# Which queue loads what in the first microseconds of a fused S5 + SwiGLU kernel on Trainium2

## The chip, the cores and the metric

The kernel runs on one core of one Trainium2 chip. A core has TensorE (PE, matrix products), VectorE (DVE), ScalarE (ACT, activation functions), GpSimd (POOL) and SyncE (SP, which here only issues DMA transfers), each with its own instruction stream. SP, ScalarE and GpSimd can each issue DMA transfers, and each has its own DMA queue. The metric is device time in microseconds (us) of one execution; the time before is the median of three runs.

## The reference

The kernel computes a layer norm of x (2048 rows of 512, bf16), and on the result a state-space layer (S5) and a SwiGLU feed-forward layer; x and both results are added.

```python
def _A_ref(x, Lambda_re, Lambda_im, B_re, B_im, C_re, C_im, log_dt, Dskip):
    Lam = Lambda_re + 1j * Lambda_im
    Bmat, Cmat = B_re + 1j * B_im, C_re + 1j * C_im
    Lam_bar = jnp.exp(jnp.exp(log_dt) * Lam)
    B_bar = ((Lam_bar - 1.0) / Lam)[:, None] * Bmat
    Bu = jnp.einsum("bld,pd->blp", x + 0j, B_bar)
    h = jnp.zeros_like(Bu[:, 0, :])
    hs = []
    for t in range(L):
        h = Lam_bar[None, :] * h + Bu[:, t, :]
        hs.append(h)
    y = 2.0 * jnp.einsum("blp,dp->bld", jnp.stack(hs, 1), Cmat).real
    return y + x * Dskip[None, None, :]

def _B_ref(x, w_gate, w_up, w_down):          # (512, 1376), (512, 1376), (1376, 512)
    return (silu(x @ w_gate) * (x @ w_up)) @ w_down

x = A_x
xn = _layernorm(x, axis=-1)
return x + _A_ref(xn, ...) + _B_ref(xn, ...)
```

Inputs and output are bf16; matrix products accumulate in f32.

## The kernel before, in words

The 2048 rows are 16 row tiles of 128, and four chunks of 512 columns of the transposed activations. The gate and up weights have 1376 columns, eleven blocks of 128 (the last of 96). They are loaded in groups of blocks: group 0 holds blocks 0 and 1, group 1 blocks 2 and 3, group 2 blocks 4 to 6, group 3 blocks 7 to 9; the last block has tiles of its own, `w_last` and `wu_last`. Everything is written in a fixed order (a manual schedule), so each engine runs its instructions in the order in which the program writes them.

For each chunk, TensorE does the gate and up products (L418), the B projection (L343), and later the down projection (L498) and the state-space output (L507). ScalarE evacuates the results from PSUM: silu on the gate (L432), a copy of the up product (L433), a copy of the B projection (L345). VectorE multiplies gate and up (L437), runs the scan and the rotations (L353 to L385) and computes the norm statistics. PSUM has eight banks, which the tiles take in turn: a tile waits until the tile eight before it has been read out.

The first 14 us are different, because nothing can start before rows, weights and norm are there. This is called the head here. The loads at its beginning (L115 to L122, with `load_w1` at L112) are split over SP's and ScalarE's queues: row tiles x0 to x3 one by one, 128 KB each, and groups 0 and 1 of gate and up, 256 KB each. After them SP issues the next four row tiles, groups 2 and 3, eight transposing loads of B, and `w_last`. Later, `load_late` (L140) puts `wu_last`, the last eight row tiles and the down weights on SP's queue. Eight semaphores are handed to these DMA transfers in turn, across both queues, and a transfer isn't issued before the earlier one with its semaphore has landed. So the ninth transfer (the next four row tiles) and those behind it wait for the head's first loads.

While the first rows load, TensorE runs `dummy` matmuls on a zero tile (L566), which keep it busy. Then, row tile by row tile: VectorE takes the statistics (L174, L599, L614), the reciprocal standard deviation comes from ScalarE's Ln and Exp for x0 (L179, L180) and from VectorE and GpSimd for the others (L183, L184), VectorE normalises (L192), TensorE transposes (L207), ScalarE copies the transposed rows to SBUF (L215; VectorE L213 for x3), and TensorE multiplies them with the first three weight blocks (`head_mm`, L591). The order at L598 to L625 interleaves the tiles; on VectorE, x1's statistics (L599) stand ahead of x0's normalisation (L600). Ln and Exp need ScalarE's function table, which is loaded once at L595; a second table load comes at L245. The pieces that the text speaks of:

```python
    allk = range(KD)
    nc.scalar.preload_act_table_set("natural_log_exp_and_others")
    dummy(10, CW)
    ln_stats(0)
    rstd_act(0)
    nc.vector.bn_stats(out=stats[:, 1, :], in_=xall[:, 1, :])
    norm_dve(0)
    ...
    xT_pe(0, 2)
    dummy(6, 128)
```

Of the kernel before, what the change touches and what calls it, by code (L numbers as in the profile page):

```python
# [23 lines left out]
def kernel(  # L24
# [17 lines left out]
    nc = tc.nc  # L42
    _, L, D = A_x.shape
    Pst = A_Lambda_re.shape[0]
    F = B_w_gate.shape[1]
    assert L % 512 == 0 and D % 128 == 0 and Pst % 128 == 0 and Pst == D
    CW = 512
# [11 lines left out]
    LA, LB = 32, 64  # L59
    FL = (FT - 1) * 128  # L60
# [18 lines left out]
    x_v = A_x[0].rearrange("(n p) d -> p n d", p=128)  # L79
    out_v = out[0].rearrange("(n p) d -> p n d", p=128)  # L80
    wg_v = B_w_gate.rearrange("(k p) f -> p k f", p=128)
    wu_v = B_w_up.rearrange("(k p) f -> p k f", p=128)


    xall = const.tile([128, NT, D], BF16, name="xall")
# [9 lines left out]
    wu_last = const.tile([128, KD, LB], BF16, name="wu_last")  # L95
# [14 lines left out]
    def load_w1(q, tiles, view, gi):  # L110
        a, b = fgroups[gi]
        q.dma_start(out=tiles[gi][:], in_=view[:, :, a * 128:min(F, b * 128)])  # L112


    nc.sync.dma_start(out=xall[:, 0, :], in_=x_v[:, 0, :])  # L115
    nc.scalar.dma_start(out=xall[:, 1, :], in_=x_v[:, 1, :])
    load_w1(nc.sync, wg_g, wg_v, 0)
    load_w1(nc.scalar, wu_g, wu_v, 0)
    nc.sync.dma_start(out=xall[:, 2, :], in_=x_v[:, 2, :])
# [18 lines left out]
    nc.sync.dma_start(out=w_last[:, :, LB + LA:128], in_=wu_v[:, :, FL:FL + LA])  # L138

    def load_late():  # L140
        nc.sync.dma_start(out=wu_last[:], in_=wu_v[:, :, FL + LA:F])
        nc.sync.dma_start(out=xall[:, 2 * TPC:NT, :], in_=x_v[:, 2 * TPC:NT, :])
        nc.sync.dma_start(out=wd_sb[:, 0:nfull, :], in_=B_w_down[0:nfull * 128, :].rearrange("(k p) d -> p k d", p=128))
        if nfull < FT:
            nc.sync.dma_start(out=wd_sb[0:LB, nfull, :], in_=B_w_down[FL + LA:F, :])
            nc.sync.dma_start(out=wd_sb[LB:LB + LA, nfull, :], in_=B_w_down[FL:FL + LA, :])
# [26 lines left out]
    def ln_stats(n):  # L173
        nc.vector.bn_stats(out=stats[:, n, :], in_=xall[:, n, :])  # L174
        nc.vector.bn_aggr(out=mv[:, n, :], in_=stats[:, n, :])
# [388 lines left out]
    def dummy(n, cols):  # L564
        for _ in range(n):
            nc.tensor.matmul(warm[:, 0:cols], lhsT=junk[:, 0:128], rhs=junk[:, 0:cols], start=True, stop=True)  # L566
# [25 lines left out]
                                 rhs=xnT[:, k, lo * 128:hi * 128], start=(k == 0), stop=(k == KD - 1))  # L592

    allk = range(KD)
    nc.scalar.preload_act_table_set("natural_log_exp_and_others")  # L595
    dummy(10, CW)
    ln_stats(0)
    rstd_act(0)  # L598
    nc.vector.bn_stats(out=stats[:, 1, :], in_=xall[:, 1, :])  # L599
# [101 lines left out]
    spread(fwd0[8:] + back0, norm2, "ssm0", "ln2")  # L701
    queue("cf", c_ops())
    load_late()
    for fi in range(G0, FT):
        gateup_tile(0, fi)
# [60 lines left out]
```

## Time and profile before

| what | value |
|---|---|
| time, median of 3 runs | 180.59 us (180.54 to 180.66) |
| the profiled execution's own time | 180.64 us |
| its span in the profile | 178.9 us |
| granted TensorE clock | 1.00 of full speed |
| PE busy | 174.0 us (97%), 919 matmuls |
| VectorE busy | 153.2 us (86%) |
| ScalarE busy | 93.8 us (52%) |
| GpSimd busy | 24.9 us (14%) |
| SP's queue (q1) | 24416 packets, 11.21 MB |
| ScalarE's queue (q10) | 1632 packets, 0.89 MB |
| read from HBM | 8.03 MB |

The span is the time from the first to the last instruction of the program that the profile shows; the rest of the execution's own time lies around it. The busy time of PE counts each matmul with a modelled end, so PE "busy" is not PE at its peak. A timeline line gives start and duration in us, the engine, the line of the kernel, the operation and its tiles; an engine with a q behind its name (SPq, ACTq) is that engine's queue issuing a DMA transfer, and the duration is that of the issue, not of the transfer. In square brackets stand the idle time before the instruction and what ended it. "To landing" is the time from the issue to the moment when the transfer's semaphore tells that all of it has arrived.

### The profile page before, as it was taken

The numbers are of one execution on the slowest core, as the hardware profiler recorded it, in microseconds if no ns is written. First come the engines' busy times: TensorE is split into PE (matmuls) and PEld (weight loads), VectorE is DVE, ScalarE is ACT, GpSimd is POOL, SyncE is SP. The second block draws the span as 40 slices with busy tenths as digits, with TensorE's granted clock in tenths as the row PEclk, the third lists the DMA queues.
The fourth block names the chain that finished last, engine by engine and source line by source line (L and its number), as shares of the span: only waits on it lengthen the run. The fifth ranks groups of instructions, "written<-read, shape, count | busy, mean of one in ns | idle before, by whom it ended". The sixth has DMA issues, their size and how long they took to land.

```text
span 178.9 us, 2463 instructions
## 1 busy us (share of the span) xinstructions
PE 174.0 (97%) x919; PEld 83.5 (47%) x919; DVE 153.2 (86%) x233; ACT 93.8 (52%) x170; POOL 24.9 (14%) x32
## 2 busy tenths in 40 slices
PE   7899999999999999999999999999999999999993
PEld 2684444443444444444444444444444444444743
DVE  2779997999999999999999999999999999950033
ACT  2479776988399957022998661014866610230000
POOL 5223000000500000027200000013405000150000
DMA  5999857994236500020930000007287900073012
GB/s 164 319 274 211 116 97 184 353 171 96 52 64 180 235 0 0 0 28 7 133 71 2 0 0 4 0 0 76 25 134 101 137 3 0 0 81 36 4 47 70
DMA packets 29515, 15.53 MB, mean 87 GB/s; under 512 B 18336, under 2 KB 29440, under 8 KB 29472
## 3 DMA queue, kind: packets, MB, share of 16 engines
q1 hardware_dynamic: 24416, 11.21, 27.3%
q0 software_dynamic: 3456, 3.28, 14.1%
q10 hardware_dynamic: 1632, 0.89, 1.8%
q8 instruction: 7, 0.11, 0.3%
q14 instruction: 4, 0.03, 0.0%
HBM read 8.03 MB, written 5.24 MB: 74 GB/s over the span
## 4 chain that ended last, share of the span: by engine, by line
PE 95%; DMA 2%; DVE 1%; ACT 0%; issue 0%
PE ps L418 36%; PE ps L498 21%; PE ps L507 15%; PE ps L343 15%; PE ps L591 3%; PE ps L444 2%; DMA xall<-in_A_x_dram 2%; PE ps L454 1%; PE ps L207 1%; DVE stats L174 0%; DVE stats L599 0%; DVE xall L192 0%; ACT xnT L215 0%; PE ps L566 0%; DVE res L510 0%
## 5 line engine op out<-in xcount | busy, mean ns | idle before, releaser
L498 PE MATMUL ps<-wd_sb,guT 128*128 128x512 bf16 (+3 forms) x198 | 38.8, 355 | 0.0
L418 PE MATMUL ps<-xnT,wg 128*128 128x512 bf16 x148 | 38.0, 379 | 0.0
L418 PE MATMUL ps<-xnT,wu 128*128 128x512 bf16 x148 | 38.0, 379 | 0.0
L385 DVE TENSOR_TENSOR_SCAN g<-r_t,car,u 128x512 bf16<-128x512 f32 x24 | 28.9, 1266 | 0.0
L507 PE MATMUL ps<-CF,wt 128*128 128x512 bf16 (+2 forms) x144 | 28.3, 355 | 0.0
L343 PE MATMUL ps<-xnT,BT 128*128 128x512 bf16 x128 | 28.3, 379 | 0.0
L498 PEld LDWEIGHTS <-guT 128*128 128x128 bf16 (+1 forms) x198 | 18.5, 98 | 19.9
L513 ACT CAST res<-ps 128x512 bf16<-128x512 f32 x12 | 7.0, 586 | 38.3 <-PE ps L507 38.3
L432 ACT ACTIVATE guT<-ps 128x512 bf16<-128x512 f32 x40 | 24.8, 620 | 3.6 <-PE ps L418 3.4
L433 ACT CAST u<-ps 128x512 bf16<-128x512 f32 x40 | 24.3, 607 | 4.1 <-PE ps L418 4.0
L514 POOL DMA_DIRECT2D out_dram<-res x12 | 11.1, 998 | 87.2 <-ACT res L513 87.2
L418 PEld LDWEIGHTS <-wu 128*128 128x128 bf16 x148 | 14.5, 98 | 17.4
L418 PEld LDWEIGHTS <-wg 128*128 128x128 bf16 x148 | 14.3, 98 | 17.6 <-issue 0.8
L507 PEld LDWEIGHTS <-wt 128*128 128x128 bf16 x144 | 13.4, 98 | 14.3
L343 PEld LDWEIGHTS <-BT 128*128 128x128 bf16 x128 | 12.5, 98 | 15.1
L345 ACT CAST u<-ps 128x512 bf16<-128x512 f32 x32 | 17.6, 590 | 2.9 <-PE ps L343 2.8
L510 DVE TENSOR_TENSOR res<-ps,xn_end 128x512 bf16<-128x512 f32 (+2 forms) x6 | 3.0, 514 | 14.4 <-PE ps L507 14.4
L437 DVE TENSOR_TENSOR guT<-guT,u 128x1024 bf16<-128x1024 bf16 x20 | 13.6, 682 | 0.0
L184 POOL TENSOR_TENSOR rstd<-ve,neg_half 128x1 f32<-128x1 f32 (+1 forms) x6 | 6.9, 1154 | 40.2 <-DVE ve L183 40.2
L174 DVE BATCH_NORM_STATS2 stats<-xall 128x6 f32<-128x512 bf16 x14 | 9.4, 670 | 2.4 <-DMA xall<-in_A_x_dram 2.4
L353 DVE TENSOR_TENSOR pm<-u,c 128x2048 bf16<-128x2048 bf16 x8 | 9.8, 1221 | 1.2 <-ACT c L270 1.1
L353 DVE TENSOR_TENSOR pm<-g,c 128x2048 bf16<-128x2048 bf16 x8 | 9.8, 1219 | 0.1
(103 smaller groups left out, 156.8 us busy)
## 6 DMA issues: line engine op xcount, KB each, us to landing
out_dram<-in_A_x_dram SPq DMA_DIRECT2D x1, 1536.0 KB, 8.5
out_dram<-res POOLq DMA_DIRECT2D x12, 128.0 KB, 3.0
out_dram<-xall POOLq DMA_DIRECT2D x3, 512.0 KB, 5.5
wd_sb<-in_B_w_down_dram SPq DMA_DIRECT2D x1, 1280.0 KB, 10.9
xall<-in_A_x_dram SPq DMA_DIRECT2D x1, 1024.0 KB, 6.5
wg<-in_B_w_gate_dram SPq DMA_DIRECT2D x2, 384.0 KB, 5.5
wu<-in_B_w_up_dram SPq DMA_DIRECT2D x2, 384.0 KB, 5.9
wu<-in_B_w_up_dram ACTq DMA_DIRECT2D x2, 256.0 KB, 5.3
```

Source lines behind the costliest of these rows:

```text
L174: nc.vector.bn_stats(out=stats[:, n, :], in_=xall[:, n, :])
L343: nc.tensor.matmul(ps[:], lhsT=BT[:, part, k, q * 128:(q + 1) * 128], rhs=xnT[:, k, c * CW:(c + 1) * CW], start=(k == 0), stop=(k == KD - 1))
L345: nc.scalar.copy(out=u_tiles[c][:, part, q, :], in_=ps[:])
L353: V.tensor_tensor(out=t[:], in0=flat(src()[:, i]), in1=flat(tab[:]), op=ALU.mult)
L385: V.tensor_tensor_scan(out=g()[:, part, q, :], data0=r_t[:, q:q + 1].to_broadcast([128, CW]), data1=u_tiles[c][:, part, q, :], initial=ini ...
L418: nc.tensor.matmul(ps[:fs, lo:hi], lhsT=wslice(groups, fi, k), rhs=xnT[:, k, c * CW + lo:c * CW + hi], start=(k == 0), stop=(k == KD - 1))
L432: nc.scalar.activation(out=guT[:fs, fi, :], in_=psg[:fs], func=ACT.Silu)
L433: nc.scalar.copy(out=u_pair[c][:fs, fi % 2, :], in_=psu[:fs])
L437: products.append(lambda: V.tensor_tensor(out=g, in0=g, in1=u, op=ALU.mult))
L498: nc.tensor.matmul(o[:], lhsT=gu_tiles[c][:fsz[fi], fi, i * 128:(i + 1) * 128], rhs=wd_sb[:fsz[fi], fi, lo:hi], start=(fi == 0), stop=False)
L507: nc.tensor.matmul(o[:], lhsT=w_tiles[c][:, part, q, i * 128:(i + 1) * 128], rhs=CF[:, part, q, lo:hi], start=False, stop=(part == 1 and q ...
L514: nc.gpsimd.dma_start(out=out_v[:, n, lo:hi], in_=res[:, lo:hi], accum_op=ALU.add)
```

## The change

The head's loads are shared out differently. The table load moves from behind ScalarE's four load issues to the very front of its stream, x1 moves from ScalarE's queue to SP's, behind x0, and so SP issues x0, x1, gate group 0, x2, gate group 1 and ScalarE issues, after the table load, up group 0, x3, up group 1. In `load_late`, `wu_last` moves from SP's queue to ScalarE's; in the built program its issue stands between the last copy of the first B projection (L345) and the silu of block 7 (L432) in ScalarE's stream. Nine dummy matmuls of 512 columns run instead of ten.

```diff
+    nc.scalar.preload_act_table_set("natural_log_exp_and_others")
     nc.sync.dma_start(out=xall[:, 0, :], in_=x_v[:, 0, :])
-    nc.scalar.dma_start(out=xall[:, 1, :], in_=x_v[:, 1, :])
+    nc.sync.dma_start(out=xall[:, 1, :], in_=x_v[:, 1, :])
     load_w1(nc.sync, wg_g, wg_v, 0)
     load_w1(nc.scalar, wu_g, wu_v, 0)
     nc.sync.dma_start(out=xall[:, 2, :], in_=x_v[:, 2, :])
...
     def load_late():
-        nc.sync.dma_start(out=wu_last[:], in_=wu_v[:, :, FL + LA:F])
+        nc.scalar.dma_start(out=wu_last[:], in_=wu_v[:, :, FL + LA:F])
         nc.sync.dma_start(out=xall[:, 2 * TPC:NT, :], in_=x_v[:, 2 * TPC:NT, :])
...
     allk = range(KD)
-    nc.scalar.preload_act_table_set("natural_log_exp_and_others")
-    dummy(10, CW)
+    dummy(9, CW)
     ln_stats(0)
```

## The prediction

> **What bounds the kernel now.** I read the busy time per stage first, then the chain that ended last, then the first 10 us of the timeline. TensorE (windows of the whole trace; after the window: its length, PE busy and count, clock, DMA share, GB/s):
>
> ```profile
> 4.60:5.60 1.00, 0.30 (x4) 1.00 1.07 280
> 6.80:7.80 1.00, 0.88 (x17) 1.00 1.07 320
> 7.80:9.80 2.00, 2.00 (x28) 1.00 1.09 350
> 12.00:60.00 48.00, 48.00 (x241) 1.00 0.77 166
> 60.00:120.00 60.00, 60.00 (x279) 1.00 0.13 23
> 120.00:176.00 56.00, 56.00 (x300) 1.00 0.38 53
> ```
>
> From 7.8 us to 176 us TensorE never pauses, so the end moves only with the moment at which that run begins, or if something makes it pause. The chain (start, us, what) says what sets that moment:
>
> ```profile
> 0.74 2.78 DMA xall<-in_A_x_dram
> 3.54 0.70 DVE stats L174
> 4.27 0.18 DVE mv L175
> 4.45 0.59 DVE stats L599
> 5.05 0.42 DVE xall L192
> 5.52 0.40 PE ps L207 x4
> ...
> 11.25 1.86 PE ps L591 x32
> 13.11 6.91 PE ps L418 x32
> ```
>
> It is the landing of x0, the first 128 rows, at 0.74 + 2.78 = 3.52 us; then statistics, ScalarE's Ln and Exp (beside x1's statistics), norm, transposes: 2.00 us from landing to the first transpose. The timeline has the issues and the consumers:
>
> ```profile
> 0.74 0.41 ACTq L116 DMA_DIRECT2D xall<-in_A_x_dram  x1
> 0.74 0.40 SPq L115 DMA_DIRECT2D xall<-in_A_x_dram  x1
> 1.18 0.46 ACTq L112 DMA_DIRECT2D wu<-in_B_w_up_dram  x1
> 1.20 0.41 SPq L112 DMA_DIRECT2D wg<-in_B_w_gate_dram  x1
> 2.77 1.28 ACT L595 ACT_TABLE_LOAD   x1 [2.77 <-issue]
> 4.49 0.29 ACT L179 ACTIVATE ve<-mv,eps_t 128x1 f32<-128x1 f32 x1 [0.43 <-DVE mv L175]
> ...
> 28.58 2.64 SPq L145 DMA_DIRECT2D wd_sb<-in_B_w_down_dram  x1
> 30.95 0.57 ACT L345 CAST u<-ps 128x512 bf16<-128x512 f32 x1
> 31.42 0.60 ACT L432 ACTIVATE guT<-ps 128x512 bf16<-128x512 f32 x1
> ```
>
> x0 and x1 leave at the same time on two queues and share the DMA engines; the table load ends at 4.05, before L179 needs it.
>
> **The change part by part.** The sum is made on the profiled execution: 180.64 us = span 178.9 + 1.74 around it; it lies 0.05 above the median, 180.59.
>
> x1 to SP, behind x0: this is the gain. Windows of the DMA give 14, 154 and 360 GB/s in 1.5 to 2.0, 2.0 to 2.5 and 2.5 to 3.0 us: 7 + 77 + 180 = 264 kB, which is x0 and x1 together (262 kB), done at about 3.0. Had x0 these bytes to itself, its 131 kB would be there at 2.5 + 47/360 = 2.63: 0.37 us earlier, landing at 3.15. A second row gives the same: the 64 KB loads on a quiet queue late in the trace (w_last, wu_last) land 2.2 us after issue; 66 kB more at 350 GB/s add 0.19, so 2.39 instead of 2.78, or 0.39. The lower end is 0: the up group takes x1's place beside x0 (if the table load doesn't hold its issue, below). I take 0.37, because in the only place of this trace where ScalarE's loads and a table load meet, the load begins 0.03 us after the last issue ends (2.29 + 0.46 = 2.75; 2.77): one after the other.
>
> Table load to the front: removed where it was free (2.77 to 4.05 with L179 waiting for L175 until 4.45). With x0's chain 0.37 earlier, L175 would be done at 4.08, so it would nearly have become the next bound; at the front (0.74 to 2.02) it is out of the way. Cost on the path 0, except that it delays ScalarE's three other loads: up group 0 from 1.18 to about 2.05, x3 from 1.67 to 2.5, up group 1 from 2.29 to 3.1.
>
> Are they late? Issue to landing was 4.4, 5.0 and 6.1 us for them, each with x1's 128 KB ahead, which now is not: at most 6.4, 7.5 and 9.2. They are needed at 6.76 (L591 on wu), 7.78 (L614) and 9.53 (L591 on wu of group 1), less 0.37: 6.39, 7.41, 9.16. Even at the upper end 0.1 late; one transfer of 128 KB fewer ahead (0.37 us at 350 GB/s) makes them early. On SP each later load is moved past one more issue, x1's (0.41): gate group 0 from 1.20 to 1.6, x2 to 2.06, gate group 1 to 2.6. By their rows (3.7, 4.1, 6.0 to landing) they land at 5.3, 6.2, 8.6, up to 0.37 more for x1's bytes; needed at 6.27, 6.76 and 8.66 less 0.37, so 5.90, 6.39, 8.29. Gate group 1 looks late, but in the trace of before all 1.57 MB of these eight loads had landed by 8.43, with the engines at a share of 1.05 or more from 2.5 us on; the order doesn't change that sum, and what ScalarE's queue moves later leaves room for SP's in front. I take 0 and keep 0.15 for the range. The later SP loads wait for semaphores of x0, x1, gate group 0 (and the first transposes of B for up group 0); all of these land no later than about 6.4, where before 5.99 was the issue of the first transpose. B is first read at 19.85, its last transpose having landed 21.2 for a use at 23.3: 2 us of cover.
>
> Nine dummies for ten: the last three stand 0.22 us apart, all end at 4.82, and PE is idle 0.70 until 5.52. Cost and gain 0: with the chain 0.37 earlier the gap is 0.55 instead of 0.33, still hidden behind x0's chain.
>
> wu_last to ScalarE: its issue (0.41 to 0.59 by the four ACTq rows) now stands between the cast at 30.95 and the silu at 31.42. Queued behind it are the silu and all evacuations; waiting for those is TensorE, through the eight banks taken in turn. The second bank of the next B projection (33.83 us) is the one which that silu frees, at 31.42 + 0.60 = 32.02: 1.81 us of cover for 0.6 us. SP's late loads start 0.62 earlier (wu_last's issue and gap); xall's second half landed at 33.9 and is read at 41.4, so no gain. wu_last itself is read at 40.73; small loads beside full DMA engines took 4.1 to 4.8 us (the parameter rows, 1 KB), so it is there by 36. Cost 0.
>
> Sum: 180.64 - 0.37 = 180.27, less 0.05 for the median, and about 0.03 back for late weights: 180.25.
>
> **A rule against it.** The trace has a semaphore record on ScalarE's queue at 159.559, while the cast that began at 159.553 ran on until 160.14: the queue ran ahead of the engine. [...]
>
> **The rivals.**
> First, the table load holds nothing. Up group 0 then leaves at about 0.8 and shares the engines with x0 as x1 did, only in smaller packets: the trace's packets take 46 ns for 1024 bytes and 25 for 512, so in turns x0 has 65% instead of 50% of an engine; its eight packets per engine save 8 x 21 = 168 ns. Time: 180.59 - 0.17 = 180.42. x1, sharing too, must land by x0 + 0.83, because its statistics (L599) stand ahead of x0's norm on VectorE; by 65% of 350 GB/s it is there about 0.6 later.
>
> Second, slower: ScalarE's issue of wu_last is held while SP's queue is full. For it: SP's issue at 28.58 took 2.64 us instead of 0.5 because its transfers were backed up, and around 31 us they still are. Against: at the start both queues issue at once, at 0.4 to 0.6 us each. A hold of d costs d - 1.81, so it decides from 1.8 + 0.37 = 2.2 us on; at 2.64 it costs 0.83 and ends at 180.25 + 0.83 = 181.1.
>
> Third, slower: a gate load is late. Gate group 0 was bounded at 5.3 to 5.7. From 6.27 on it takes the whole gain back; at 6.62, 0.9 past the bound, the first matmuls start 0.35 later than before: 180.59 + 0.35 = 180.94. For it: x1 is ahead of it now and up group 0 may run beside it; against: it had 1.35 us in hand (4.92 against 6.27).
>
> Fourth: one dummy fewer lets the clock fall back. Dummies took 0.43 us apart until 3.7 and 0.22 after; head matmuls at half speed would cost up to 1.5 us: 181.7. Against it: a gap of 0.70 was harmless.
>
> **How the numbers follow.** Forecast (x0 alone) 0.44, own range 180.05 to 180.45; first rival 0.32; the three slower ones 0.13, 0.08, 0.03. No change to within 0.2% (about what a measurement of this kernel can tell) is 180.23 to 180.95. The forecast lies at that edge: 0.28 of its 0.44 beyond it if the landing gains a little more than 0.37, 0.16 within. The first rival: 0.06 faster, 0.24 within, 0.02 slower. The slower ones: 0.22 slower, 0.02 within. Sum: 0.34 faster, 0.42 same, 0.24 slower. The range reaches from 179.95 (landing 0.64 earlier) to 180.95; about 0.16 lies above and 0.04 below.
>
> **What would show it.** In the profile after: ScalarE's first DMA issue at 2.0 or at 0.8; x0's statistics at 3.15 to 3.2 (before 3.54), the first transpose 2.0 later; the run of L591 without a pause on a weight load; ScalarE's issue near 31 us under 0.7 us long, and PE at 100% in 12 to 176 us. A PE idle time there, or a first transpose after 5.5, makes me wrong.

## The result, and the profile after

The changed kernel takes 181.19 us (median of 16 executions, 181.10 to 181.68), the kernel before beside it 180.66 (16 executions). The ratio is 1.0029, with a 95% interval of 1.0022 to 1.0037: 0.3% slower, 0.9 us above the forecast of 180.25 and outside its range. The profiled execution of the changed kernel is one of its longer ones: 181.56 us, span 179.8; TensorE's last matmul ends 0.92 us later in it than in the profile of before, while the medians are 0.53 apart.

The chain that ended last (start, us, what) no longer runs through x0's landing:

```profile
1.20 0.41 SPq L117
1.65 5.38 DMA wg<-in_B_w_gate_dram
7.08 0.84 PE ps L592 x12
...
8.49 1.54 PE ps L592 x20
```

The same two pieces of TensorE's work in the chain of the kernel before:

```profile
6.27 0.88 PE ps L591 x12
...
7.72 1.54 PE ps L591 x20
```

The load in the chain after is gate group 0, issued at 1.65 us and landed at 1.65 + 5.38 = 7.03; in the kernel before it landed at 4.92. The timeline of the changed kernel has the issues and the consumers (start, us, engine, line, operation; in brackets the idle time before and what ended it):

```profile
0.74 1.28 ACT L115 ACT_TABLE_LOAD   x1 [0.74 <-PEq L750]
0.74 0.40 SPq L116 DMA_DIRECT2D xall<-in_A_x_dram  x1
0.77 0.46 ACTq L112 DMA_DIRECT2D wu<-in_B_w_up_dram  x1
1.20 0.41 SPq L117 DMA_DIRECT2D xall<-in_A_x_dram  x1
1.25 0.53 ACTq L121 DMA_DIRECT2D xall<-in_A_x_dram  x1
1.65 0.43 SPq L112 DMA_DIRECT2D wg<-in_B_w_gate_dram  x1
...
3.03 0.69 DVE L175 BATCH_NORM_STATS2 stats<-xall 128x6 f32<-128x512 bf16 x1 [1.87 <-DMA xall<-in_A_x_dram]
...
4.66 0.69 DVE L599 BATCH_NORM_STATS2 stats<-xall 128x6 f32<-128x512 bf16 x1 [0.72 <-DMA xall<-in_A_x_dram]
...
5.73 0.45 PE L208 MATMUL ps<-ident,xall 128*128 128x128 bf16 x4 [0.51 <-DVE xall L193]
...
7.08 0.62 PE L592 MATMUL ps<-xnT,wg 128*128 128x128 bf16 x8 [0.56 <-DMA wg<-in_B_w_gate_dram]
...
7.69 0.69 DVE L175 BATCH_NORM_STATS2 stats<-xall 128x6 f32<-128x512 bf16 x1 [0.64 <-DMA xall<-in_A_x_dram]
```

Three loads are waited for. x0's statistics do start 0.51 us earlier (3.03 for 3.54). But VectorE then waits 0.72 us for x1, whose statistics stand ahead of x0's norm, and the first transpose comes at 5.73 instead of 5.52. TensorE then waits 0.56 us for gate group 0 and begins its first products at 7.08 instead of 6.27. x2's statistics wait too, until 7.69. And ScalarE's first load was issued at 0.77, in the middle of the table load.

Two of the windows that the prediction shows (TensorE's busy time after its window's length, with its count; then the same for its weight loads, VectorE, ScalarE and GpSimd; at the end of a line TensorE's clock, the DMA share and GB/s):

```profile
6.80:7.80 1.00, 0.72 (x13) 0.73 (x14) 0.36 (x2) 0.00 (x0) 0.00 (x0) 1.00 1.09 303
7.80:9.80 2.00, 1.88 (x31) 1.67 (x28) 1.85 (x6) 0.65 (x2) 0.56 (x1) 1.00 1.09 344
```

In 6.8 to 7.8 us TensorE is busy for 0.72 instead of 0.88, and in 7.8 to 9.8 us for 1.88 instead of 2.00. TensorE's delay against the profile of before grows in three places: 0.77 us when the run begins (8.49 for 7.72), 0.08 more at x2's transposes (9.94 for 9.10), 0.07 more at 34.6 us. From there to the end it stays at 0.92.

**Where the loads went.** The packet records tell, by queue and packet size (1024 bytes for x, 512 for these weights), when half of a load's bytes had been moved (the packets of one queue and size counted in order). In us:

| load | before: queue, issue | half there | landed | after: queue, issue | half there | landed |
|---|---|---|---|---|---|---|
| x0 | SP 0.74 | 2.58 | 3.52 | SP 0.74 | 2.40 | 3.00 |
| up 0 | ScalarE 1.18 | 4.25 | 5.56 | ScalarE 0.77 | 3.14 | 4.28 |
| x1 | ScalarE 0.74 | 2.79 | 3.74 | SP 1.20 | 3.75 | 4.64 |
| x3 | ScalarE 1.67 | 5.41 | 6.62 | ScalarE 1.25 | 4.09 | 5.06 |
| gate 0 | SP 1.20 | 3.46 | 4.92 | SP 1.65 | 4.71 | 7.03 |
| up 1 | ScalarE 2.29 | 6.71 | 8.43 | ScalarE 1.81 | 5.51 | 7.90 |
| x2 | SP 1.65 | 4.88 | 5.77 | SP 2.13 | 6.01 | 7.67 |
| gate 1 | SP 2.20 | 6.22 | 8.22 | SP 2.68 | 6.74 | 8.61 |

Sort the changed kernel's loads by issue: the half times rise in the same order, over both queues. The loads were moved in one line, in the order in which they were issued. The kernel before shows the same, two by two. Its line was the order of need (x0, x1, the two groups 0, x2, x3, the two groups 1). The change takes an entry off ScalarE's queue, so all that ScalarE loads moves up by one place, and adds one to SP's, so all that SP loads moves back: up group 0 before x1, x3 (needed last of the rows) before gate group 0, up group 1 before x2.

The line can be seen in the queues' packets. Kernel before, 2.7 to 3.2 us (queue: packets, MB, share of the 16 engines; q1 is SP's queue, q10 ScalarE's):

```profile
DMA packets 257, 0.17 MB, mean 340 GB/s; under 512 B 31, under 2 KB 257, under 8 KB 257
q1 hardware_dynamic: 168, 0.09, 66.3%
q10 hardware_dynamic: 89, 0.08, 44.0%
```

The changed kernel, same window:

```profile
DMA packets 232, 0.12 MB, mean 238 GB/s; under 512 B 0, under 2 KB 232, under 8 KB 232
q10 hardware_dynamic: 232, 0.12, 94.2%
```

x1 had been issued at 1.20, but SP's queue moves nothing in this window: ScalarE's up group 0 has the engines to itself, at 238 GB/s instead of the 340 of both. The size of the delay is near that: between gate group 0 and its old place stand up group 0 and x3, 393 kB; the mean of the half-microsecond windows from 2.5 to 4.5 us is 309 GB/s; 393 / 309 = 1.27 us, and its half time moved by 4.71 - 3.46 = 1.25.

### The profile page after: what moved, and what is told of

It is laid out like the page before. It is cut to its first block, busy times and chain, and to the rows that moved or that the text cites. A ratio compares the mean times of both kernels' runs of the same rounds, so it can differ in the third digit from the quotient of the medians.

```text
span 179.8 us, 2445 instructions
## 1 busy us (share of the span) xinstructions
PE 173.7 (97%) x902; PEld 83.4 (46%) x918; DVE 153.3 (85%) x233; ACT 93.4 (52%) x170; POOL 24.9 (14%) x32
## 3 DMA queue, kind: packets, MB, share of 16 engines
q0 software_dynamic: 3456, 3.28, 14.3%
## 4 chain that ended last, share of the span: by engine, by line
PE 94%; DMA 3%; issue 1%; SPq 0%; ACT 0%; DVE 0%
PE ps L419 35%; PE ps L499 21%; PE ps L344 15%; PE ps L508 15%; PE ps L592 3%; DMA wg<-in_B_w_gate_dram 3%; PE ps L445 2%; PE ps L455 1%; PE ps L208 0%; SPq L117 0%; SPq L116 0%; ACT xnT L216 0%; DVE res L511 0%; PE ps L237 0%
## 5 line engine op out<-in xcount | busy, mean ns | idle before, releaser
L499 PE MATMUL ps<-wd_sb,guT 128*128 128x512 bf16 (+4 forms) x195 | 38.6, 355 | 0.2
L419 PE MATMUL ps<-xnT,wu 128*128 128x512 bf16 x146 | 37.5, 379 | 0.1
```

Source lines behind the costliest of these rows:

```text
L419: nc.tensor.matmul(ps[:fs, lo:hi], lhsT=wslice(groups, fi, k), rhs=xnT[:, k, c * CW + lo:c * CW + hi], start=(k == 0), stop=(k == KD - 1))
L499: nc.tensor.matmul(o[:], lhsT=gu_tiles[c][:fsz[fi], fi, i * 128:(i + 1) * 128], rhs=wd_sb[:fsz[fi], fi, lo:hi], start=(fi == 0), stop=False)
```

## The experiments

All times are medians beside executions of the kernel before on the same chip. "PE late" is the end of TensorE's last matmul against the profile of before; "tail" is from the end of VectorE's last instruction to the end of the span. Both are of the one profiled execution, whose head can lie nearly half a microsecond from another's (see the end). Landings in us; "-" where the trace doesn't tell it.

| kernel | us | before | ratio, 95% | PE late | tail | x1 | gate 0 | up 0 | x2 |
|---|---|---|---|---|---|---|---|---|---|
| after | 181.19 | 180.66 | 1.0029, 1.0022 to 1.0037 | 0.92 | 2.5 | 4.64 | 7.03 | 4.28 | 7.67 |
| x1_only | 181.72 | 180.57 | 1.0064, 1.0052 to 1.0076 | 0.62 | 3.0 | 4.72 | 6.72 | 4.16 | 7.43 |
| order_only | 181.70 | 180.57 | 1.0066, 1.0053 to 1.0078 | 0.48 | 3.0 | 4.66 | 6.51 | 4.11 | 7.30 |
| wulast_only | 180.90 | 180.57 | 1.0019, 1.0009 to 1.0028 | 0.11 | 2.7 | 3.69 | 4.79 | 5.44 | 6.16 |
| dummy9_only | 180.63 | 180.57 | 1.0002, 0.9993 to 1.0012 | -0.08 | 2.5 | 3.61 | 4.87 | 6.06 | 6.70 |
| sp_plus1 | 181.56 | 180.73 | 1.0043, 1.0030 to 1.0056 | 0.25 | 3.5 | 3.51 | 4.89 | 5.83 | - |
| held | 182.09 | 180.73 | 1.0092, 1.0057 to 1.0127 | 1.26 | 2.4 | 3.31 | 4.84 | 6.12 | 5.27 |
| x3_first | 181.83 | 180.73 | 1.0067, 1.0040 to 1.0093 | 1.33 | 2.5 | 3.81 | 7.46 | 4.77 | 8.14 |
| all_sp | 180.57 | 180.73 | 0.9986, 0.9974 to 0.9997 | -0.11 | 2.5 | 3.42 | 4.91 | 5.79 | 6.27 |
| gate_first | 181.28 | 180.60 | 1.0034, 1.0022 to 1.0047 | 0.56 | 2.5 | 4.57 | 4.19 | 6.02 | 7.38 |
| swap_queues | 182.88 | 180.60 | 1.0119, 1.0095 to 1.0142 | 1.82 | 2.4 | 5.15 | 7.34 | 4.34 | 8.18 |
| held_wu1 | 180.99 | 180.60 | 1.0015, 1.0003 to 1.0027 | 0.17 | 2.5 | 3.31 | 5.07 | 6.22 | 5.54 |
| all_sp8 | 180.34 | 180.60 | 0.9990, 0.9978 to 1.0001 | -0.45 | 2.4 | 3.27 | 4.75 | 5.63 | 6.36 |
| norm_first | 181.34 | 180.80 | 1.0028, 1.0017 to 1.0040 | 0.75 | 2.5 | 4.58 | 6.84 | 4.23 | 7.57 |
| gate_x2 | 181.42 | 180.80 | 1.0040, 1.0028 to 1.0053 | 0.77 | 2.5 | 4.46 | 4.08 | 7.48 | 5.25 |
| all_sp8_x2 | 180.93 | 180.80 | 1.0016, 1.0004 to 1.0028 | 0.17 | 2.4 | 3.34 | 5.38 | 6.87 | 5.58 |

### The change in its parts

**x1_only**: the kernel before, with x1's load moved to SP and nothing else.

```diff
-    nc.scalar.dma_start(out=xall[:, 1, :], in_=x_v[:, 1, :])
+    nc.sync.dma_start(out=xall[:, 1, :], in_=x_v[:, 1, :])
```

> Before, with x1 moved to SP behind x0; the table load stays behind ScalarE's loads. Theory (the table load holds nothing, so its place doesn't matter; up group 0 is issued first on ScalarE at 0.74): as slow as the head of the changed kernel or slower, 181.0 to 181.6 us, gate group 0 again after 6.5. Rival (the table load at the front is what costs): 180.6 or below.

**order_only**: the changed kernel with ten dummies and `wu_last` on SP again, so x1 on SP and the table load in front.

```diff
-    dummy(9, CW)
+    dummy(10, CW)
-        nc.scalar.dma_start(out=wu_last[:], in_=wu_v[:, :, FL + LA:F])
+        nc.sync.dma_start(out=wu_last[:], in_=wu_v[:, :, FL + LA:F])
```

> Only the head's loads as in the change (table load first, x1 on SP); ten dummies and wu_last on SP as before. Theory (the transfers are served in the order of their issue over both queues, so that up group 0, issued at 0.77 us, stands ahead of x1 and gate group 0): nearly the whole loss, 181.0 to 181.2 us; x1 lands near 4.6 us, gate group 0 near 7.0, the first L592 matmul near 7.1. Rival (the loss comes from wu_last on ScalarE or from the missing dummy): 180.6 or below.

The move of x1 alone does it: in both, x1 lands at 4.7, gate group 0 at 6.5 to 6.7, and TensorE is 0.48 to 0.62 us late. Up group 0 was issued at 0.74 in the one and at 0.77 in the other, so the table load's place makes no difference. Both are slower than the changed kernel itself, though TensorE is less late in them. What they lose more lies behind the work, in the column "tail": 3.0 us instead of 2.5.

**sp_plus1**: the kernel before with a load of 64 bytes more on SP, to see that end by itself.

```diff
         nc.sync.dma_start(out=wu_last[:], in_=wu_v[:, :, FL + LA:F])
+        extra = const.tile([1, 32], BF16, name="extra")
+        nc.sync.dma_start(out=extra[:], in_=B_w_down[0:1, 0:32])
```

> The kernel before, with one more load of 64 bytes on SP's queue behind wu_last's (into a tile that nothing reads). It asks for the end of the program: with x1 moved to SP, and the rest as before, the time rose by more than TensorE's delay, and about 0.4 us of it lay behind the last output's landing. Theory (the count of SP's instructions sets it): TensorE as before to 0.1 us, the span 0.4 to 0.5 longer, behind the last landing; 181.0 to 181.2 us. Rival (the end follows from something else in those runs): no change, 180.4 to 180.8.

The tail is 1.0 us longer, more than expected, and the time 0.8 us. SP's closing instructions are in the trace's records: in the kernel before two drains follow each other at 177.99 and 178.05 us; in order_only they stand at 178.47 and 178.96, and SP's stream arrives later at the end. x1_only and order_only have one SP instruction more than the kernel before; the changed kernel has as many as before (x1 more, `wu_last` less), and its tail is the old one. So 0.5 us of these two runs belongs to a side effect that the changed kernel doesn't have. It doesn't grow with the count: with one instruction less (wulast_only) the tail is 0.2 longer, with four more (the all_sp runs) or two less (swap_queues) it is shorter, by less than 0.1.

**wulast_only**: the kernel before with `wu_last` on ScalarE's queue.

```diff
-        nc.sync.dma_start(out=wu_last[:], in_=wu_v[:, :, FL + LA:F])
+        nc.scalar.dma_start(out=wu_last[:], in_=wu_v[:, :, FL + LA:F])
```

> Before, with wu_last on ScalarE's queue alone. Theory: ScalarE's issue is held while SP's queue is backed up, ScalarE is idle some 1.6 us near 32 us, and TensorE loses 0 to 0.1 us at the second bank of the next B projection: 180.6 to 180.75 us. Rival (this is the loss): 181.0 or more.

The time rises by 0.19%, 0.34 us, more than expected; the tail has 0.2 of it. The timeline shows the hold on ScalarE, and the weight load for which TensorE waits, at a cost of 0.09:

```profile
32.40 0.39 ACTq L141 DMA_DIRECT2D wu_last<-in_B_w_up_dram  x1
32.83 0.60 ACT L432 ACTIVATE guT<-ps 128x512 bf16<-128x512 f32 x1 [1.28 <-DMA xall<-in_A_x_dram]
40.77 0.57 PEld L454 LDWEIGHTS <-wu_last 128*64 128x64 bf16 x8 [0.51 <-DMA wu_last<-in_B_w_up_dram]
```

The issue waits for its semaphore, which the second half of x had before it: that landed at 32.38, and `wu_last` was issued at 32.40. The silu behind it starts 1.28 us after the cast has ended, and TensorE doesn't stop for it. But `wu_last`, on a queue of its own, takes 8.3 us and lands at 40.73 (28.97 in the kernel before, issued on SP at 26.79). TensorE's first product with it starts 0.40 us behind the product ahead of it, instead of 0.31.

In the changed kernel the second half of x landed at 33.48, so the hold is longer:

```profile
33.50 0.40 ACTq L142 DMA_DIRECT2D wu_last<-in_B_w_up_dram  x1
33.94 0.60 ACT L433 ACTIVATE guT<-ps 128x512 bf16<-128x512 f32 x1 [1.58 <-PE ps L445]
```

The cast before it ended at 32.36. (The bracket names a product of TensorE; what the silu stood behind is the issue, 0.02 us after x's landing in all nine runs with `wu_last` on ScalarE.) The bank is free at 34.54, and TensorE, which would have used it at 34.52, goes on at 34.59: 0.07 us lost. `wu_last` lands at 40.41, in time for 41.59.

**dummy9_only**: the kernel before with nine dummies.

```diff
-    dummy(10, CW)
+    dummy(9, CW)
```

> Before, with nine dummies. Theory: nothing, 180.6 us within 0.1. Rival (one dummy fewer lets TensorE's clock come later or fall back): 180.9 or more, with head matmuls over 0.25 us apart per 512 columns.

No difference.

### Is it the place in the line?

**held**: the changed kernel, with up group 0's issue held until the table load has ended, which is what the forecast had assumed (`seed` is one element, set to zero by VectorE).

```diff
     nc.scalar.preload_act_table_set("natural_log_exp_and_others")
+    nc.scalar.activation(out=wu_g[0][0:1, 0, 0:1], in_=seed[:], func=ACT.Exp)
     nc.sync.dma_start(out=xall[:, 0, :], in_=x_v[:, 0, :])
```

> The changed kernel, with one edit: a one-element Exp on ScalarE, behind the table load, writes the first element of up group 0's tile, so that up group 0's load can be issued only once the table load (0.74 to 2.02 us) has ended. Theory (the loads of both queues are served in order of issue): up group 0 is issued at about 2.2 us, x0 lands at 3.0, x1 at 3.4 to 3.8 instead of 4.64, gate group 0 at 4.6 to 5.2 instead of 7.03, up group 0 at 5.3 to 6; the first transpose comes 0.4 to 0.5 us earlier than before's 5.52, the first matmul of the gate at or before 6.27, and the time is 180.0 to 180.4 us, that is what the prediction had forecast. Rival (SP's queue alone is slow, whatever ScalarE's queue carries): x1 and gate group 0 land within 0.3 us of 4.64 and 7.03, and the time stays at 181.0 to 181.3.

The landings came as the theory said: x1 3.31, gate group 0 4.84, and TensorE's first products began 0.57 us earlier than in the kernel before. But the time is 1.4 us longer than before, a miss; the timeline shows where:

```profile
3.15 0.51 SPq L130 DMA_DIRECT2D xall<-in_A_x_dram  x1
3.28 0.46 ACTq L112 DMA_DIRECT2D wu<-in_B_w_up_dram  x1
10.78 0.61 PE L595 MATMUL ps<-xnT,wu 128*128 128x256 bf16 x4 [1.75 <-DMA wu<-in_B_w_up_dram]
```

With x0 landed early, SP could issue the next 512 KB of x at 3.15, and up group 1 at 3.28 stood behind it in the line: it landed at 10.74. Half of its bytes had been moved at 8.51, for 6.71 before.

**held_wu1**: the same, with up group 1 on SP behind gate group 1.

```diff
-    load_w1(nc.scalar, wu_g, wu_v, 1)
+    load_w1(nc.sync, wu_g, wu_v, 1)
-    nc.sync.dma_start(out=w_last[:, :, LB + LA:128], in_=wu_v[:, :, FL:FL + LA])
+    nc.gpsimd.dma_start(out=w_last[:, :, LB + LA:128], in_=wu_v[:, :, FL:FL + LA])
```

> The run in which up group 0's issue was held until after the table load, with up group 1 on SP's queue behind gate group 1, so that it is issued before x's second quarter (one small load of w_last goes to GpSimd's queue, so that SP's instructions are as many as before). The held run began 0.57 us earlier than the kernel before but lost 1.8 us where up group 1 landed at 10.74, having been issued at 3.28, just behind SP's 512 KB of x at 3.15. Theory (that place in the order was the whole loss): up group 1 lands at 8.4 to 9.2, TensorE runs on without that wait, 0.3 to 0.57 us earlier than the kernel before: 180.1 to 180.4. Rival (loads held back at the start are late anyhow): another wait of 0.5 us or more before 12 us, 180.9 or more.

Up group 1 lands at 9.04 and that wait is gone, as the theory has it. The time, 180.99, is not what it gave. All that it has over the kernel before, 0.39 us, lies outside the span: here the time exceeds the span by 2.13 to 2.21 us in each of the 11 executions, in every execution of the other runs by 1.72 to 1.84, and the median span is that of the kernel before, 178.8. This is the only run with one more load on GpSimd's queue; whether that is the cause wasn't tried. Inside the span the early start isn't kept either: in the profiled execution it was lost to matmuls at half speed, which the last section comes back to.

**x3_first**: ScalarE's loads in the order x3, up group 0, up group 1.

```diff
-    load_w1(nc.scalar, wu_g, wu_v, 0)
     nc.scalar.dma_start(out=xall[:, 3, :], in_=x_v[:, 3, :])
+    load_w1(nc.scalar, wu_g, wu_v, 0)
```

> The changed kernel with ScalarE's loads in the order x3, up group 0, up group 1. Theory (order of issue): x3, in 1024-byte packets, takes the place of up group 0 beside x0; x1 then waits behind 131 kB of it instead of up group 0's 262 kB in 512-byte packets and lands at 3.6 to 4.0 us instead of 4.64; gate group 0 then at 6.0 to 6.6, up group 0 after it at 6.3 to 7; time 180.6 to 181.0. Rival (x1 is late because it is second on its own queue, whatever ScalarE's loads are): x1 within 0.2 us of 4.64, time 181.0 to 181.4.

x1 lands at 3.81, as the line has it. The rest was missed: gate group 0 has half of its bytes at 4.67, but lands at 7.46, up group 0 is ahead of it, and the time is 181.83. The line explains the half times of all eight loads here too (x0 2.25, x3 2.74, x1 3.12, up 0 3.72, gate 0 4.67, up 1 5.52, x2 5.90, gate 1 6.72), not how long the rest of a load takes. From half to landing gate group 0 took 1.5 us in the kernel before and 1.0 in held and all_sp, where SP's own loads follow it; with up group 1 of the other queue right behind it, it took 1.8 to 2.8 (order_only, norm_first, after, x3_first). What draws the end out is open; it makes up about 0.9 of gate group 0's 2.1 us in the changed kernel's profile.

**swap_queues**: the eight loads of the changed kernel, ScalarE's on SP and SP's on ScalarE.

```diff
-    nc.sync.dma_start(out=xall[:, 0, :], in_=x_v[:, 0, :])
-    nc.sync.dma_start(out=xall[:, 1, :], in_=x_v[:, 1, :])
-    load_w1(nc.sync, wg_g, wg_v, 0)
-    load_w1(nc.scalar, wu_g, wu_v, 0)
+    nc.scalar.dma_start(out=xall[:, 0, :], in_=x_v[:, 0, :])
+    nc.scalar.dma_start(out=xall[:, 1, :], in_=x_v[:, 1, :])
+    load_w1(nc.scalar, wg_g, wg_v, 0)
+    load_w1(nc.sync, wu_g, wu_v, 0)
     ...
```

> The changed kernel with the two queues exchanged for the eight head loads, in the same order (ScalarE: x0, x1, gate 0, x2, gate 1; SP: up 0, x3, up 1). Theory (order of issue decides, whichever queue): x1 lands at 4.4 to 4.9 us, up group 0 at 4.1 to 4.5, gate group 0 at 6.5 to 7.2, as in the changed kernel; TensorE 0.5 to 1.0 us late. Rival (ScalarE's queue goes ahead of SP's): x1 lands before up group 0, at 3.4 to 3.8, gate group 0 by 5, and TensorE is earlier than in the kernel before. The time may carry another end on SP, which has two instructions fewer; the landings decide.

Gate group 0 is late here too (7.34), up group 0 early (4.34), so ScalarE's queue has no right of way. TensorE is 1.82 us late, more than the 0.5 to 1.0 expected: up group 0 now stands ahead of x0 as well (landed 4.00) and x1 (5.15), the first transpose comes 0.71 us late, and the products ran at half speed up to about 9.5 us (0.107 us apart; the last section has more on it).

**all_sp**: all eight loads on one queue, so the line is written down in the program.

```diff
     nc.sync.dma_start(out=xall[:, 0, :], in_=x_v[:, 0, :])
     nc.sync.dma_start(out=xall[:, 1, :], in_=x_v[:, 1, :])
     load_w1(nc.sync, wg_g, wg_v, 0)
-    load_w1(nc.scalar, wu_g, wu_v, 0)
+    load_w1(nc.sync, wu_g, wu_v, 0)
     nc.sync.dma_start(out=xall[:, 2, :], in_=x_v[:, 2, :])
-    nc.scalar.dma_start(out=xall[:, 3, :], in_=x_v[:, 3, :])
+    nc.sync.dma_start(out=xall[:, 3, :], in_=x_v[:, 3, :])
     load_w1(nc.sync, wg_g, wg_v, 1)
-    load_w1(nc.scalar, wu_g, wu_v, 1)
+    load_w1(nc.sync, wu_g, wu_v, 1)
```

(Ten dummies, and `wu_last` on SP.)

> The changed kernel with all eight head loads on SP's queue in the order in which they are needed (x0, x1, gate group 0, up group 0, x2, x3, gate group 1, up group 1), ten dummies, wu_last on SP; ScalarE issues no load at the start. Theory (order of issue): x0 lands at 2.6 to 3.0 us, x1 at 3.0 to 3.5, gate group 0 at 4.2 to 5, up group 0 at 5 to 5.8; TensorE's run begins 0.4 to 0.7 us earlier than before (7.72), and the time is 180.0 to 180.3, plus about 0.43 if the four more instructions on SP bring the same longer end on SP that the runs with one more instruction on SP showed (180.4 to 180.7). Rival (one queue alone moves data too slowly, as up group 0 alone ran at 230 GB/s in the changed kernel): gate group 0 after 6 us, up group 1 after 9.5, time 181.3 or more.

x0 lands at 2.89, x1 at 3.42, gate group 0 at 4.91, up group 1, the last of the eight, at 8.75 (8.43 before): one queue is enough. At 180.57 us it is 0.14% faster than the kernel before beside it, less than expected, since another bound stands right behind (timeline):

```profile
1.19 4.39 PE L567 MATMUL ps<-junk 128*128 128x512 bf16 x10 [1.19 <-DVE eps_t L157]
5.42 0.39 PE L208 MATMUL ps<-ident,xall 128*128 128x128 bf16 x4
```

x0's norm had ended at 4.83, but the ten dummies ran until 5.58.

**all_sp8**: the same with eight dummies.

```diff
-    dummy(10, CW)
+    dummy(8, CW)
```

> The run with all eight head loads on SP's queue in order of need, with eight dummies instead of ten. With ten, x0's norm ended at 4.83 us but the dummies, all at 0.43 us apart, ran to 5.58, so the first transpose waited. Theory: the dummies end at about 4.65, the first transpose comes at 4.9 to 5.0 instead of 5.42, gate group 0 (4.91) is in time, TensorE's run begins 0.4 to 0.6 us earlier than in the kernel before: 180.0 to 180.3 us. Rival (fewer dummies delay TensorE's full speed, or up group 0 and x2 now bound): the gain stays below 0.2 us, 180.4 to 180.8.

The first transpose comes at 4.75, TensorE's products begin 0.77 us earlier than before, and 0.31 is given back where x2 (6.36) is waited for. The median is 0.26 us below that of the kernel before, but the interval just takes in 1. The two versions can't be told from each other; they are the only ones here whose median is below that of both kernels.

### What the three late loads cost

**norm_first**: the changed kernel with x1's statistics behind x0's norm.

```diff
-    nc.vector.bn_stats(out=stats[:, 1, :], in_=xall[:, 1, :])
     norm_dve(0)
+    nc.vector.bn_stats(out=stats[:, 1, :], in_=xall[:, 1, :])
```

> The changed kernel with x1's statistics moved behind x0's norm on VectorE, so that x1's late landing (4.64) no longer holds x0's norm. Theory (gate group 0's landing, not x1's, sets when TensorE's run begins, so x1's 0.21 us of delay lies under gate group 0's wait): the first transpose at 4.9 to 5.2 us instead of 5.73, the first gate matmul still at gate group 0's landing, 6.5 to 7.1, TensorE and the time as in the changed kernel to 0.15 us, 181.05 to 181.35. Rival (x1's delay costs by itself): 0.2 us or more earlier than the changed kernel, 180.7 to 181.0.

```profile
5.01 0.63 PE L208 MATMUL ps<-ident,xall 128*128 128x128 bf16 x4
6.88 0.62 PE L592 MATMUL ps<-xnT,wg 128*128 128x128 bf16 x8 [0.60 <-DMA wg<-in_B_w_gate_dram]
```

The transposes come 0.72 us earlier than in the changed kernel, and the products still wait for gate group 0. The ratio is 1.0028, that of the changed kernel. x1's delay costs nothing there: it lies under gate group 0's.

**gate_first**: gate and up exchanged between the queues.

```diff
-    load_w1(nc.sync, wg_g, wg_v, 0)
-    load_w1(nc.scalar, wu_g, wu_v, 0)
+    load_w1(nc.sync, wu_g, wu_v, 0)
+    load_w1(nc.scalar, wg_g, wg_v, 0)
     ...
-    load_w1(nc.sync, wg_g, wg_v, 1)
-    load_w1(nc.scalar, wu_g, wu_v, 1)
+    load_w1(nc.sync, wu_g, wu_v, 1)
+    load_w1(nc.scalar, wg_g, wg_v, 1)
```

> The changed kernel with gate and up exchanged between the queues: gate groups 0 and 1 on ScalarE's queue, where up groups 0 and 1 were, and these on SP's. It parts the changed kernel's loss into x1's share and gate group 0's. Theory (transfers of both queues are served nearly in order of issue; gate group 0 came late because it was issued fifth, at 1.65): gate group 0, issued at 0.77 us, lands at about 4.3, up group 0 at about 7.0, x1 still at about 4.6; the first gate matmul follows the first transposes without a wait, at 6.4 to 6.6, up group 0 costs at most 0.3; TensorE's delay is 0.2 to 0.5 us less than in the changed kernel: 180.75 to 181.0 us. Rival (gate weights come late whichever queue carries them, because the engines are full): gate group 0 after 6, time 181.1 or more.

```profile
6.41 0.66 PE L592 MATMUL ps<-xnT,wg 128*128 128x128 bf16 x8
7.40 0.69 DVE L175 BATCH_NORM_STATS2 stats<-xall 128x6 f32<-128x512 bf16 x1 [0.41 <-DMA xall<-in_A_x_dram]
9.65 0.40 PE L208 MATMUL ps<-ident,xall 128*128 128x128 bf16 x4 [0.25 <-DVE xall L193]
```

The gate is there at 4.19 and the products begin 0.14 us late, without a wait. Then x2, landed at 7.38, holds its statistics, and at its transposes TensorE is 0.56 late. The time, 181.28, is above the 180.75 to 181.0 expected; against the changed kernel nothing is gained (1.0034): when gate group 0 is early, x2 takes its place.

**gate_x2**: the same with x2 ahead of up group 0 on SP.

```diff
+    nc.sync.dma_start(out=xall[:, 2, :], in_=x_v[:, 2, :])
     load_w1(nc.sync, wu_g, wu_v, 0)
-    nc.sync.dma_start(out=xall[:, 2, :], in_=x_v[:, 2, :])
```

> The run with gate and up exchanged, and in it x2 issued ahead of up group 0 on SP's queue (x0, x1, x2, up 0, up 1; ScalarE as there: gate 0, x3, gate 1). With the gate early, TensorE was 0.14 us late at the first gate matmul and then 0.42 more at x2's transposes, x2 having landed at 7.38. Theory (x2 is the third late load, hidden under gate group 0's wait in the changed kernel): x2 lands at 5.3 to 6.3, up group 0 at 6.2 to 7.0, just in time; TensorE 0.1 to 0.35 us late, 180.7 to 181.0. Rival (another load becomes late by as much, as the bytes ahead stay the same): 181.1 or more.

```profile
7.53 0.40 PE L592 MATMUL ps<-xnT,wu 128*128 128x128 bf16 x4 [0.51 <-DMA wu<-in_B_w_up_dram]
```

x2 is early (5.25), and up group 0 is late (7.48). The rival of this run held: what one load gains another loses.

**all_sp8_x2**: all_sp8 with x2 ahead of up group 0.

```diff
+    nc.sync.dma_start(out=xall[:, 2, :], in_=x_v[:, 2, :])
     load_w1(nc.sync, wu_g, wu_v, 0)
-    nc.sync.dma_start(out=xall[:, 2, :], in_=x_v[:, 2, :])
```

> The run with all head loads on SP and eight dummies, with x2 ahead of up group 0 (x0, x1, gate 0, x2, up 0, x3, gate 1, up 1). There TensorE began 0.77 us earlier than in the kernel before and gave 0.31 back at x2's transposes, x2 having landed at 6.36. Theory: x2 lands at 5.4 to 5.8, up group 0 at 6.0 to 6.4, where it was first used at 6.0, so at most 0.3 is lost there; TensorE 0.5 to 0.75 earlier than before where its full speed has come by 4.8 us, 180.0 to 180.3. Rival (what x2 gains, up group 0 loses): 180.3 to 180.6.

The same again, in the other order: x2 at 5.58, up group 0 at 6.87 with a wait of 0.62 us. At 180.93 (1.0016) it loses more than the rival gave; gate group 0 is later too (5.38 for 4.75 in all_sp8). The place of x2 behind up group 0, which the kernel before has too, is the better one.

## Why the prediction was wrong

- **What bounds the kernel**: right. TensorE ran on after the head in all runs, so the time followed the moment at which its run begins (in gate_first TensorE is 0.56 us late at x2's transposes, 9.65 us, and 0.56 at its last matmul).
- **x1 to SP, gain 0.37**: x0's part was right, and larger (landing 3.00 for 3.52). The first step that failed stands in the sentence on the lower end, and in the first rival: a load beside x0 was taken to share the engines with it and x1 packet by packet, with x1 about 0.6 us after x0. The loads stand in line instead; x1 landed 1.64 us after x0. The condition written there, that x1 must land within 0.83 us of x0, was the right question with the wrong price. (The packets of 512 bytes, put at 25 ns there, took 27 in the median, which changes little.)
- **Table load to the front**: its own cost of 0 holds (x1_only and order_only differ by less than either's interval), but it holds no issue: 0.77, in the middle of 0.74 to 2.02. The reading that was taken, one after the other because they stood so in the trace of before, mistook the order in the program for a wait. The first rival had this right, and the semaphore record at 159.559 pointed to it: ScalarE's queue went on there while a cast ran until 160.14, as it does here during the table load. held shows that the assumption would have brought the early start, 0.57 us.
- **Are the weights late? 0, keep 0.15**: this is the step that failed and decides the result. Gate group 0 was bounded at 5.3 to 5.7 by adding its old 3.7 us to its new issue. That row had been measured two places further ahead in the line. It took 5.4 and landed at 7.03 (6.5 to 7.0 in the four runs with this order), needed at 5.90. "The order doesn't change that sum" is true of the last landing (8.61 for 8.43) and says nothing on which load is late. The sign named for being wrong came with it: the first transpose at 5.73, and the products with a pause on a weight load. With the line, the trace of before would have given it: 393 kB more ahead at its own 0.5 us windows of 249 to 360 GB/s is 1.1 to 1.6 us more.
- **Third rival, a late gate load**: this is what happened. Its price was worked out for 6.62 as 180.94; the landings were 6.5 to 7.0 and the time 181.19. The mechanism was right, its landing too early, and its chance of 0.08 too low.
- **B's transposing loads, issued later**: right, TensorE waits for none of them; its delay is the same before and at the first use of B (0.84 us at 9.94, 0.85 at 20.70).
- **Nine dummies, 0**: right (1.0002).
- **`wu_last`, 0**: the second rival's hold is real, but not because SP's queue is full: the issue waits for the second half of x, whose semaphore it has (33.48, issued 33.50). Why SP's issue at 28.58 took 2.64 us (2.50 in the changed kernel, at 28.19) no run shows; that its transfers were backed up was the author's reading. The cover was read as 1.81 us from 33.83, where the trace of before has the end of a matmul; the second bank's first matmul starts at 33.66, so the cover was 1.64. The silu came 1.68 late (33.94 for 31.42, less TensorE's own 0.84), so the cost is 0.07 instead of 0. "There by 36" failed too: `wu_last` landed at 40.41, which costs nothing in the changed kernel and 0.09 in wulast_only. By itself the move costs 0.34 us, about half of it at SP's end, which the prediction didn't consider and the changed kernel doesn't show.
- **PE at 100% in 12 to 176 us**: the changed kernel's profile reads less, 47.74 of 48.00 us in 12 to 60. Only the 0.07 is a delay; at the other places a matmul's record is missing (as at 35.45, where the next starts 0.432 us later, twice 0.216), and TensorE's delay stays what it was.
- **Fourth rival, the clock**: not by the dummies (dummy9_only, 1.0002). But the moment of full speed varies, 3.9 to 6.9 us in five profiles, below.

The sum with what was measured, in the changed kernel's profile: gate group 0's landing 0.77, x2's 0.08, `wu_last`'s hold 0.07, together 0.92. Where gate group 0 lands half a microsecond earlier, as in order_only's profile, TensorE is 0.48 late instead, 0.25 of it when the run begins and the rest at x2's transposes. The medians' 0.53 would fit such an execution; no profile shows one of the changed kernel.

## What to carry to other kernels

While the DMA engines are full (in both kernels a share of 0.98 or more in each half microsecond from 2.5 to 8.5 us), write the loads of all queues into one list by their time of issue, add up the bytes ahead of each, and compare the list with the order of need; moving one load to another queue moved every later load on both here, its half time by 0.5 to 1.3 us. A duration from issue to landing belonged to a place in that list and couldn't be taken along to another: gate group 0 took 3.72 us in its old place and 5.38 in the new one. Ask, too, which semaphore an issue waits for, and what stands behind it on the issuing engine (`wu_last` was issued 0.02 us after the second half of x had landed, and the silu stood behind it). When one late load is brought forward, look for the next one: here the wait went from gate group 0 (landed 7.03) to x2 (7.38 in gate_first) to up group 0 (7.48 in gate_x2), and only the order of need left none that cost much.

## What the runs showed that was not expected

**One line for two queues.** In the changed kernel SP's queue moved nothing from 2.7 to 3.2 us although x1 had been issued at 1.20; in the profiles of all 17 kernels, half of each of the eight loads was there in the order of issue over both queues (loads issued within 0.03 us of each other aside). `wu_last` shows it far from the head: alone on ScalarE's queue, issued at 33.50 in the changed kernel, it had half of its bytes moved at 38.95, while four loads that SP had issued by 31.4 us landed at 37.17 to 39.06. The first rival's estimate let a load on each queue share the engines packet by packet. These traces don't agree for loads issued some tenths of a microsecond apart (up group 0, issued at 0.77 in the changed kernel, had half of its bytes moved at 3.14, x1, issued at 1.20, at 3.75); x0 and x1 of the kernel before, issued together at 0.74, did run side by side, with half moved at 2.58 and 2.79. Turns by whole loads are a rival, since they would give the eight loads the same order in most runs, where the queues' issues alternate. Against them speak `wu_last` and held, where x2 (SP, 2.13) went ahead of up group 0 (ScalarE, 2.27) right behind gate group 0 (SP); no run was made to decide it.

**When TensorE comes to full speed.** The heads of the kernel before and of sp_plus1 are the same code, but their dummies and transposes aren't. Timeline of the kernel before:

```profile
1.19 3.63 PE L566 MATMUL ps<-junk 128*128 128x512 bf16 x10 [1.19 <-DVE eps_t L156]
5.76 0.50 PE L566 MATMUL ps<-junk 128*128 128x128 bf16 x6
```

Timeline of sp_plus1:

```profile
1.19 4.45 PE L568 MATMUL ps<-junk 128*128 128x512 bf16 x10 [1.19 <-DVE eps_t L158]
5.43 0.63 PE L209 MATMUL ps<-ident,xall 128*128 128x128 bf16 x4
5.86 0.85 PE L568 MATMUL ps<-junk 128*128 128x128 bf16 x6
```

Matmuls of 128 columns follow each other at 0.055 us in the one and at 0.107 in the other. By that spacing full speed came at 3.9 us in the profile of before, 4.1 in order_only, 5.8 in the changed kernel, 6.6 in sp_plus1, 6.9 in held_wu1; the windows' clock column says 1.00 throughout. In held_wu1 this took back the early start: its transposes came at 5.04, 0.48 us before those of the kernel before, but 0.107 us apart, and by the twelfth product TensorE was 0.17 late, which it stayed. So the moment differs by 2.7 us between two profiles of the same head (3.9 and 6.6); what sets it no run shows. That bounds what one profile of a head can tell: TensorE's delay differs by 0.25 us between these two, and by 0.44 between order_only and the changed kernel, where gate group 0's landing differs as well. The medians have to decide.

**The end of SP's stream.** One small load more on SP lengthened the time behind the last work by 0.5 to 1.0 us, one less by 0.2, two less or four more not at all. The cause wasn't settled; a change of a load's queue can carry this with it, and it showed only in the time from the last instruction to the end of the span.
